# Who issues the loads of V's neighbouring rows in a block-sparse attention and FFN kernel: sync engine or GpSimd

## The chip, the cores and the metric

One core of one Trainium2 chip runs the whole program. The metric is device time in microseconds (us), the median of the runs. Engines are named as in the profile: PE (TensorE matmul), PEld (its weight loads), DVE (VectorE), ACT (ScalarE), POOL (GpSimd), SP (SyncE, which here only issues DMAs).

## What is computed

The reference is attention over blocks of 32 tokens followed by a two-matrix feed-forward net. It is cut here to its core:

```python
B, H, S, D = 4, 8, 768, 64          # 24 blocks of 32 tokens
scores = (q @ k.T) / sqrt(D)
mask = |blk_i - blk_j| <= 1  or  blk_i, blk_j in (first, last)  or  blk_j in sampled_blocks[blk_i]   # 3 per block
attn = softmax(where(mask, scores, -1e9))
x = (attn @ v).transpose(0, 2, 1, 3).reshape(B * S, H * D)      # 3072 x 512
out = leaky_relu(x @ w_in, 0.01) @ w_out                        # 512 -> 2048 -> 512
```

Inputs are f32, and the FFN weights come in a 64-bit type (the kernel reads them as pairs of 32-bit words and decodes them). Every f32 operand is split into a high and a low f16 part so that PE works in f16.

## The kernel before, in words

The program is one long list of instructions without loops at run time. The work is cut by batch b (4), by query tile T (12 of 64 queries each: tile 0 holds the first and the last block and sees all keys, tiles 1 to 11 hold two inner blocks) and by pair of heads hp (4). Four tiles make an item of 256 queries, and each item's attention output goes through the FFN later.

For an inner tile the keys and values are put together in 12 slots of 32 rows, 384 rows in all. Slots 0 to 3 are the four neighbouring blocks, contiguous in memory. Slots 4 to 9 are the sampled blocks, and slots 10 and 11 are the first and the last block. For K this is done in SBUF: DVE copies the neighbours (L631), POOL copies the six sampled blocks (`kg`, L640, each after a register load L639). For V it is done by DMA out of a scratch tensor `scr[b]` in DRAM, which holds V of that batch as f16 high and low parts, one row of 2048 bytes for each token (written by SP at L496 from `prep_v`).

`gather_v(b, T)` fills one of two buffers `vg` (128 partitions x 3 chunks x 2048 bytes), used in turn:

- L659: chunk 0, the 128 neighbouring rows, a plain DMA of 256 KB, for every inner tile (44 times);
- L663: the first and the last block into chunk 2, 32 rows each, only the first time that a buffer is used for a batch (16 times);
- L666: two indirect DMAs by GpSimd with the row numbers in `rows`, 128 rows into chunk 1 and 64 rows into chunk 2 (88 times).

A buffer can be refilled when the attention-times-V matmuls (`av`, L798) of the tile that used it are done; both the plain and the indirect loads wait for that.

What sets the order: the kernel writes its instructions down step by step with priorities, and the framework's scheduler then makes one fixed order for each engine out of dependencies, priorities and its own estimate of durations. Each engine works through its list strictly in order, so an instruction that waits holds up all that stands behind it on that engine. SP's list holds all plain loads and stores and all transposes by DMA: weights (L344), q and k (L516, L526), v (L465), the transposes of k (L558), of q (L583, followed by the two swapped copies `qxs`, L586 and L587) and of the probabilities (`pt`<-`pp`, L771). POOL's list holds the `kg` copies, the indirect loads, for item 0 the diagonal matrices `pp` (L738) with which PE transposes probabilities (`turn`, L756), and later the low half of the FFN's hidden values (`g`, L847).

Other lines that the prediction speaks of: the decoding of weights on ACT (L351) and DVE (L352, L353, L355), their split into halves on ACT (L414) and DVE (L419), the masked scores on DVE (`p`, `mx`, L706), the low half of q (`qa_q`, L580) and of the probabilities (`pt` at L760 for item 0, `pp` at L766 after it), the FFN matmuls on PE (`h` L833, `o` L860). The load of a piece of the weights is ordered behind the latest `pt` transpose on SP (L345).

Of the kernel before, what the change touches and what calls it, by code (L numbers as in the profile page):

```python
# [19 lines left out]
P = 128  # L20
# [48 lines left out]
def tile_block_sparse_attention_ffn(  # L69
# [19 lines left out]
    nc = tc.nc  # L89
# [369 lines left out]
    vscale, vraw, v16s, scr, vg = {}, {}, {}, {}, {}  # L459
# [194 lines left out]
    def gather_v(b, T):  # L654

        n = (b * (NT - 1) + T - 1) % 2
        vg = vgb[n]
        t0 = (T - 1) * Q2
        nc.sync.dma_start(out=vg[:, 0, :], in_=scr[b][t0:t0 + P, :])  # L659
        if vends.get(n) != b:  # L660
            vends[n] = b
            for i, at in enumerate((0, S - BLOCK)):
                nc.sync.dma_start(  # L663
                    out=vg[Q2 + i * BLOCK:Q2 + (i + 1) * BLOCK, 2, :], in_=scr[b][at:at + BLOCK, :])
        for c, n_ in ((1, P), (2, Q2)):
            nc.gpsimd.indirect_dma_start(  # L666
                out=vg[:n_, c, :], out_offset=None, in_=scr[b][:, :],
                in_offset=bass.IndirectOffsetOnAxis(ap=rows[:n_, c - 1, T - 1:T], axis=0))
        vgs[b, T] = vg.rearrange("p c (h x) -> p c h x", h=H)
# [364 lines left out]
    def start_gather_v():  # L1034
        b, T = vq.popleft()
        until(("v", b), lambda: (b, "ready") in scr)
        assert vfree[0] > 0
        if not b and T == 1:
            build_rows()
        vfree[0] -= 1  # L1040
        gather_v(b, T)
# [73 lines left out]
    for u in units:  # L1115
        it, ui = u.item, u.k * NP + u.hp
        b, nb = it.b, it.b + 1
# [172 lines left out]
```

## Time and profile before

| what | value |
| --- | --- |
| median of the runs | 863.69 us |
| the profiled execution, whole | 867.32 us |
| its span (first to last instruction) | 865.6 us |
| PE busy | 745.7 us (86%) |
| DVE busy | 601.8 us (70%) |
| ACT busy | 509.9 us (59%) |
| POOL busy | 356.3 us (41%), of it 94.2 in the 88 indirect loads |
| queue of SP (hardware_dynamic) | 116.74 MB, 64.9% of 16 DMA engines' span |
| queue of POOL (software_dynamic) | 17.31 MB, 8.2% |

How to read it: the profile gives for each engine its busy time and, in views by window, how that is spread over the span. The view of waits says for an idle stretch which instruction ended it ("engine line waited for: us in total, times, longest us"; SPq and POOLq are the issuing queues). The timeline lists instructions in order: start, length, engine, line, operation, with the idle time before it and what ended it in square brackets. A row of an issuing queue has the time that the issue took, not the transfer.

### The profile page before, as it was taken

The page shows a single profiled execution, that of the slowest core. Times are in us where ns is not written, and L with a number is a line of the kernel's source. Part 1 is how long each engine was busy: PE and PEld are TensorE (multiplying, and loading weights), DVE is VectorE, ACT ScalarE, POOL GpSimd, SP SyncE. Part 2 cuts the span into 40 slices and gives each one's busy share as a digit, 9 for nine tenths or more (in the row PEclk, how much of TensorE's full clock was granted, in tenths as well). Part 3 has the DMA queues.
Part 4 walks back from the last instruction along what each step waited for, and adds up shares of the span by engine and source line. Part 5 has one row for each costly group of instructions (what it writes and reads, how often), then busy time and mean ns, then how long its engine had stood idle before and what let it go on. Part 6 is the DMA issues. An engine that isn't in the chain of part 4 may idle for free.

```text
span 865.6 us, 20081 instructions
## 1 busy us (share of the span) xinstructions
PE 745.7 (86%) x7140; PEld 494.9 (57%) x7140; DVE 601.8 (70%) x1595; ACT 509.9 (59%) x1183; POOL 356.3 (41%) x473
## 2 busy tenths in 40 slices
PE   1456667766998899998999989999999999999997
PEld 1245545443756565665666566666666666666674
DVE  4668998988968678757966777778667676663221
ACT  4556676775634667666656757667467566553211
POOL 0416744642125346345543554453434554532121
PEclk9968979887999999999999999999999999999999
DMA  9877489998648879898759899967678576566000
GB/s 205 162 225 237 160 191 230 234 216 181 137 104 145 172 163 211 160 170 147 194 124 177 159 162 203 199 133 183 144 131 175 116 158 148 120 139 86 26 2 25
DMA packets 312771, 135.33 MB, mean 156 GB/s; under 512 B 279773, under 2 KB 292062, under 8 KB 312670
## 3 DMA queue, kind: packets, MB, share of 16 engines
q1 hardware_dynamic: 307038, 116.74, 64.9%
q0 software_dynamic: 5632, 17.31, 8.2%
q8 instruction: 56, 0.92, 0.5%
q14 instruction: 45, 0.37, 0.1%
HBM read 65.58 MB, written 12.58 MB: 90 GB/s over the span
## 4 chain that ended last, share of the span: by engine, by line
PE 43%; DVE 20%; DMA 18%; ACT 8%; issue 5%; SPq 3%; POOL 1%; POOLq 1%; ACTq 0%; DVEq 0%
PE o L860 17%; PE h L833 17%; PE av L798 4%; PE s L697 4%; DMA kt<-k_k 3%; DVE pp L766 3%; ACT p L718 3%; DVE p L706 3%; DMA rq<-in_q_dram 3%; DMA qs_q<-qa_q 3%; DMA qxs_q<-qs_q 2%; DMA pt<-pp 2%; DMA wbuf<-in_moe_w_out_dram 2%; DVE ht L842 1%; DMA rk<-in_k_dram 1%
## 5 line engine op out<-in xcount | busy, mean ns | idle before, releaser
L860 PE MATMUL o<-W,g 128*128 128x512 f16 x1152 | 273.8, 383 | 9.3 <-DVE g L846 6.7
L833 PE MATMUL h<-x,W 128*128 128x256 f16 x2304 | 276.0, 277 | 1.9 <-ACT ht L839 1.9
L833 PEld LDWEIGHTS <-W 128*128 128x128 f16 x2304 | 223.9, 100 | 49.0 <-issue 14.2
L847 POOL TENSOR_TENSOR g<-ht,g 128x512 f16<-128x512 f32 x96 | 116.4, 1213 | 312.7 <-DVE g L846 279.1
L860 PEld LDWEIGHTS <-g 128*128 128x128 f16 x1152 | 108.2, 98 | 132.4 <-issue 15.0
L718 ACT ACTIVATE p<-p,mx 128x384 f32<-128x384 f32 x208 | 126.1, 607 | 98.0 <-DVE mx L706 66.7
L640 POOL COPY kg<-kt 128x256 f16 x264 | 133.1, 531 | 76.6 <-PE s L697 42.6
L766 DVE SCALAR_TENSOR_TENSOR pp<-p,r,pp 128x384 f16<-128x384 f32 x188 | 125.3, 694 | 33.1 <-ACT pp L745 32.4
L666 POOL DMA_INDIRECT vg<-scr,rows x88 | 94.2, 1071 | 69.5 <-PE av L798 47.4
L842 DVE SCALAR_TENSOR_TENSOR ht<-ht 128x512 f32<-128x512 f32 x96 | 67.8, 706 | 75.2 <-ACT ht L839 75.0
L706 DVE CUSTOM_DVE_ANT_0 p<-s,em,nsc 128x384 f32<-128x384 f32 x176 | 102.9, 610 | 21.9 <-PE s L697 17.3
L745 ACT ACTIVATE pp<-p,r 128x384 f16<-128x384 f32 x188 | 104.1, 604 | 17.1 <-DVE r L730 15.6
L798 PE MATMUL av<-pt,vg 128*64 128x128 f16 x2112 | 80.8, 225 | 19.7 <-DMA pt<-pp 13.6
L798 PEld LDWEIGHTS <-vg 128*64 128x64 f16 x2112 | 68.3, 112 | 49.1 <-issue 43.9
L839 ACT ACTIVATE ht<-h,gd 128x512 f32<-128x512 f32 x80 | 54.1, 677 | 63.9 <-PE h L833 51.0
L697 PE MATMUL s<-kg,qs_q 128*64 128x384 f16 x352 | 60.7, 343 | 21.5 <-DVE mx L706 21.2
L697 PE MATMUL s<-kg,qxs_q 128*64 128x384 f16 x352 | 60.0, 336 | 6.1 <-DMA qxs_q<-qs_q 6.1
L697 PEld LDWEIGHTS <-qs_q 128*64 128x64 f16 x416 | 26.9, 110 | 55.5 <-issue 43.5
L846 DVE CAST g<-ht 128x512 f16<-128x512 f32 x96 | 42.3, 441 | 10.3 <-PE o L860 8.3
L730 DVE RECIPROCAL r<-sum 128x2 f32<-128x2 f32 x96 | 15.4, 160 | 36.3 <-ACT sum L729 35.6
L718 ACT ACTIVATION_READ_ACCUMULATOR p<-p,mx 128x1 f32 x208 | 39.1, 188 | 0.0
L571 ACT ACTIVATE qa_q<-rq 128x512 f16<-128x512 f32 x25 | 15.7, 628 | 38.8 <-DMA rq<-in_q_dram 38.8
(136 smaller groups left out, 762.1 us busy)
## 6 DMA issues: line engine op xcount, KB each, us to landing
vg<-scr SPq DMA_DIRECT2D x44, 256.0 KB, 3.8
qxs_q<-qs_q SPq DMA_DIRECT2D x48, 128.0 KB, 2.6
v<-in_v_dram SPq DMA_DIRECT2D x32, 192.0 KB, 4.8
scr<-v SPq DMA_DIRECT2D x16, 384.0 KB, 4.7
W<-in_moe_w_in_dram SPq DMA_DIRECT2D x5, 1024.0 KB, 9.4
rq<-in_q_dram SPq DMA_DIRECT2D x20, 256.0 KB, 6.1
out_dram<-ob SPq DMA_DIRECT2D x20, 256.0 KB, 3.1
rk<-in_k_dram SPq DMA_DIRECT2D x24, 192.0 KB, 4.7
```

The source lines that it names most:

```text
L640: nc.gpsimd.tensor_copy(out=kg[:, :, slot * BLOCK:(slot + 1) * BLOCK], in_=kt[:, :, bass.ds(off, BLOCK)])
L666: nc.gpsimd.indirect_dma_start(out=vg[:n_, c, :], out_offset=None, in_=scr[b][:, :], in_offset=bass.IndirectOffsetOnAxis(ap=rows[:n_, c - ...
L697: nc.tensor.matmul(o, a, k, start=(n == 0), stop=(n == 1)))
L706: nc.vector.tensor_tensor_reduce(out=u.p[i], in0=u.sp[i], in1=kgs[u.b, u.T][1] if u.T else zero.to_broadcast([P, KEYS]), scale=u.nsc, scal ...
L718: nc.scalar.activation(u.p[i], u.p[i], AF.Exp, scale=-1.0, bias=u.mx[:, :1], accum_out=u.pair.sum[:, u.pi, i:i + 1])
L745: nc.scalar.activation(pp[:, 0, :], p, AF.Copy, scale=u.r)
L766: nc.vector.scalar_tensor_tensor(out=pp[:, 1, :], in0=p, scalar=u.r, in1=pp[:, 0, :], op0=ALU.mult, op1=ALU.subtract)
L798: nc.tensor.matmul(o, a, m, start=(c == 0 and l == 0), stop=(c == n - 1 and l == 1)))
L833: nc.tensor.matmul(c.ph[:, i], w, x, start=(d == 0 and m == 0), stop=(d == NP - 1 and m == 2)))
L842: nc.vector.scalar_tensor_tensor(out=c.t, in0=c.t, scalar=0.01, in1=c.t, op0=ALU.mult, op1=ALU.max)
L847: nc.gpsimd.tensor_tensor(out=c.g[:, 1], in0=c.t, in1=c.g[:, 0], op=ALU.subtract)
L860: nc.tensor.matmul(o, a, w, start=(c.first and i == 0 and m == 0), stop=(c.last and i == 1 and m == 2)))
```

## The change

Three lines of `gather_v`: the neighbouring rows and the two end blocks are issued by GpSimd instead of the sync engine. Bytes, buffers, shapes and dependencies stay as they are.

```diff
         t0 = (T - 1) * Q2
-        nc.sync.dma_start(out=vg[:, 0, :], in_=scr[b][t0:t0 + P, :])
+        nc.gpsimd.dma_start(out=vg[:, 0, :], in_=scr[b][t0:t0 + P, :])
         if vends.get(n) != b:
             vends[n] = b
             for i, at in enumerate((0, S - BLOCK)):
-                nc.sync.dma_start(
+                nc.gpsimd.dma_start(
                     out=vg[Q2 + i * BLOCK:Q2 + (i + 1) * BLOCK, 2, :], in_=scr[b][at:at + BLOCK, :])
```

60 issues leave SP's list and join POOL's. Since the scheduler makes its order anew, other instructions change places as well; the order in which FFN matmuls stand between the attention tiles on PE is nearly the same.

First place: POOL at the first two gathers of batch 0 (T = 1 and 2). `vg_100` and `vg_101` are the two buffers, `scr_564` the scratch of batch 0, `pp_...<-eye` the diagonals for PE's transposes, and rows L639 (register loads) between the copies. Before:

```order
L738 TENSOR_SCALAR pp_0_0_3_511<-eye_88,r_0_0_2_490 128x128
L666 DMA vg_100<-scr_564,rows 128x1024
L666 DMA vg_100<-scr_564,rows 64x1024
L666 DMA vg_101<-scr_564,rows 128x1024
L666 DMA vg_101<-scr_564,rows 64x1024
L640 ISA
L640 COPY kg_98<-kt_136 128x8x32
```

and now:

```order
L738 TENSOR_SCALAR pp_0_0_3_511<-eye_88,r_0_0_2_490 128x128
L659 DMA vg_100<-scr_564 128x1024
L663 DMA vg_100<-scr_564 32x1024 x2
L666 DMA vg_100<-scr_564,rows 128x1024
L666 DMA vg_100<-scr_564,rows 64x1024
L659 DMA vg_101<-scr_564 128x1024
L663 DMA vg_101<-scr_564 32x1024 x2
L666 DMA vg_101<-scr_564,rows 128x1024
L666 DMA vg_101<-scr_564,rows 64x1024
L640 ISA
L640 COPY kg_98<-kt_136 128x8x32
```

Ten issues in a row instead of four stand ahead of the `kg` copies and, behind five of these, of the next diagonals.

Second place: DVE at the first scores of tile T = 2, which wait for PE's transposes and so for those diagonals (`W<-W,wi_s` is the split of a piece of the weights, `qa_q_1_0` the low half of q of item 1). Before:

```order
L154 RECIPROCAL wi_s<-wi_inv 128x1
L706 ISA p_0_2_0_0_765,mx_0_2_0_766<-s_0_2_0_0_719,em_2_715,nsc_0_1_0_717 128x384
L706 ISA mx_0_2_0_766 128x1
L154 RECIPROCAL q_1_0_s<-q_1_0_inv 128x1
L598 TENSOR_SCALAR nsc_1_0_0_1221<-kinv_132,q_1_0_inv 128x4
L816 TENSOR_TENSOR x_0_999<-xf_0_0_2_929,x_0_999 128x4x64
L706 ISA p_0_2_1_0_855,mx_0_2_1_856<-s_0_2_1_0_720,em_2_715,nsc_0_1_0_717 128x384
```

and now:

```order
L154 RECIPROCAL wi_s<-wi_inv 128x1
L154 RECIPROCAL q_1_0_s<-q_1_0_inv 128x1
L598 TENSOR_SCALAR nsc_1_0_0_1221<-kinv_132,q_1_0_inv 128x4
L816 TENSOR_TENSOR x_0_999<-xf_0_0_2_929,x_0_999 128x4x64
L419 SCALAR_TENSOR_TENSOR W<-W,wi_s 128x2x512
L580 SCALAR_TENSOR_TENSOR qa_q_1_0_830<-rq_1_0_668,q_1_0_s,qa_q_1_0_830 128x8x64
L706 ISA p_0_2_0_0_765,mx_0_2_0_766<-s_0_2_0_0_719,em_2_715,nsc_0_1_0_717 128x384
```

One split of weights and the low half of q now stand ahead of the scores, where they stood behind them.

Third place: SP from the weight loads behind the first gathers on. Before:

```order
L659 DMA vg_101<-scr_564 128x1024
L663 DMA vg_101<-scr_564 32x1024 x2
L344 DMA W<-in_moe_w_in_dram 128x2x1024
L344 DMA W<-in_moe_w_out_dram 128x2x1024
L344 DMA W<-in_moe_w_in_dram 128x2x1024
L583 DMA_TRANSPOSE qs_q_1_0_968<-qa_q_1_0_830 128x8x128
```

and now:

```order
L496 DMA scr_564<-v_0_3_729 128x6x256
L344 DMA W<-in_moe_w_in_dram 128x2x1024
L344 DMA W<-in_moe_w_out_dram 128x2x1024
L583 DMA_TRANSPOSE qs_q_1_0_968<-qa_q_1_0_830 128x8x128
L516 DMA rq_1_1_973<-in_q_dram 128x8x64
L586 DMA qxs_q_1_0_970<-qs_q_1_0_968 64x1024
L587 DMA qxs_q_1_0_970<-qs_q_1_0_968 64x1024
L344 DMA W<-in_moe_w_in_dram 128x2x1024 x2
```

The issues for `vg` are gone, and the third load of weights has moved behind the transpose and the copies of q.

## The prediction

> **What bounds the kernel now.** I read the page's busy tenths first, then windows cut where they change, then the waits of PE, and last the timeline where PE still waits. The tenths (40 slices of about 21.6 us):
>
> ```profile
> PE   1456667766998899998999989999999999999997
> DVE  4668998988968678757966777778667676663221
> ```
>
> PE is short of work for about ten slices and full from there on, while DVE is fullest in slices 4 to 9. The windows say the same in numbers:
>
> ```profile
> core 0: us, PE busy (x) PEld busy (x) DVE busy (x) ACT busy (x) POOL busy (x), PEclk, DMA share, GB/s
> ...
> 60.00:75.00 15.00, 12.72 (x123) 10.30 (x124) 10.92 (x36) 8.98 (x21) 9.48 (x14) 0.75 0.80 251
> 75.00:100.00 25.00, 14.75 (x163) 11.60 (x163) 24.66 (x45) 18.13 (x41) 16.20 (x20) 0.93 0.57 185
> 100.00:125.00 25.00, 15.44 (x191) 11.76 (x190) 25.00 (x72) 17.36 (x37) 15.77 (x18) 0.80 0.65 158
> 125.00:250.00 125.00, 97.29 (x894) 64.69 (x892) 108.09 (x274) 82.95 (x182) 43.29 (x48) 0.90 0.91 198
> 250.00:600.00 350.00, 326.58 (x3229) 212.74 (x3228) 255.14 (x679) 224.91 (x545) 160.76 (x224) 0.99 0.82 163
> 600.00:865.60 265.60, 258.90 (x2416) 169.18 (x2414) 144.88 (x366) 128.05 (x301) 98.81 (x125) 1.00 0.53 109
> ```
>
> From 75 to 125 us DVE works 49.66 of 50 us (it decodes weights and does the scores), from 125 to 250 still 108.09 of 125. After 250 us PE sets the pace: it idles 350 - 326.58 = 23.4 us and 265.6 - 258.9 = 6.7 us. PE's work is fixed and full at the end, so the end moves by as much as the start of that full stretch moves. What happens before 250 us counts; what happens after it counts only where PE itself waits. PE's waits, from 60 to 250 us and behind it:
>
> ```profile
> PE av L798 <- DMA pt<-pp: 13.6, 7, 4.7
> ...
> PE turn L756 <- POOL pp L738: 2.5, 3, 1.4
> ...
> PE turn L756 <- POOL kg L640: 1.8, 1, 1.8
> ...
> PE s L697 <- DMA qxs_q<-qs_q: 1.7, 2, 0.9
> ```
>
> ```profile
> PE s L697 <- DMA qxs_q<-qs_q: 4.4, 4, 1.9
> ...
> PE av L798 <- DMA pt<-pp: 3.1, 3, 1.8
> ...
> PE o L860 <- POOL g L847: 0.7, 1, 0.7
> ```
>
> No row has PE waiting for `vg`: the transfers that the change touches are early enough. What can move the time is their issuing, by freeing SP or by loading POOL.
>
> **What it takes off SP.** The issues themselves are short, and their cost to SP is the wait for `av` in front of them, since SP is in order. Over the span, and from 60 to 250 us:
>
> ```profile
> SPq L659 <- PE av L798: 89.7, 23, 14.5
> ```
>
> ```profile
> SPq L659 <- PE av L798: 28.6, 4, 14.5
> ```
>
> 61.1 of the 89.7 us lie outside the stretch from 60 to 250 us, where SP has to serve a PE that is nearly full anyway. Of the 28.6 us, the largest part is one place:
>
> ```profile
> 86.58 0.43 SPq L344 DMA_DIRECT2D wbuf<-in_moe_w_out_dram  x1
> 101.33 11.37 SPq L659 DMA_DIRECT2D vg<-scr  x2
> 113.13 1.96 SPq L771 DMA_TRANSPOSE pt<-pp  x1
> 115.14 1.00 SPq L344 DMA_DIRECT2D W<-in_moe_w_in_dram  x1
> ```
>
> ```profile
> 112.50 0.60 DVE L766 SCALAR_TENSOR_TENSOR pp<-p,r,pp 128x384 f16<-128x384 f32 x1
> ```
>
> SP stands from 87 to 112.7 us behind two loads for `vg`. Next in its list is the transpose of `pp`, and DVE finishes that `pp` only at 113.1; the weight load behind it is ordered behind that transpose by the code. So freeing SP here gains nothing: the wait for `av` becomes a wait for `pp` of the same end. Term: 0. Its bounds are 0 and the whole of what PE waits for `pt` and `qxs` behind 60 us, 13.6 + 1.7 + 4.4 + 3.1 = 22.8 us; I take the end that the one long wait shows, and keep the other for a rival.
>
> One load moves the wrong way. The third of these weight loads was issued at 68.62, and now stands behind the transpose of q:
>
> ```profile
> 68.62 0.47 SPq L344 DMA_DIRECT2D W<-in_moe_w_in_dram  x1
> 80.98 1.24 SPq L583 DMA_TRANSPOSE qs_q<-qa_q  x1
> ```
>
> ```profile
> 87.75 1.14 ACT L351 ACTIVATE W<-W 128x1024 f32<-128x1024 f32 x1 [1.02 <-DVE W L355]
> ```
>
> Its decoding starts on ACT no earlier than 87.75, and what that waits for is DVE, not the load. I put it at 0, since the decoding moves later by the term below; without that cover it would cost the few us by which the load then lands too late.
>
> **What it puts on POOL.** The trace before has no plain load issued by POOL. The nearest row is the indirect issue of the same engine into the same buffer; the issues by SP bound it from below:
>
> ```profile
> L666 POOL DMA_INDIRECT vg<-scr,rows x88: 899/1000/1943, 62.9 to 788.4; - x88
> L659 SPq DMA_DIRECT2D vg<-scr x44: 326/356/1367, 62.0 to 786.7; - x44
> L663 SPq DMA_DIRECT2D vg<-scr x16: 372/420/1542, 62.4 to 650.8; - x16
> ```
>
> Where it matters most is the first double gather, because work that others wait for is queued behind it:
>
> ```profile
> 62.90 1.33 POOL L666 DMA_INDIRECT vg<-scr,rows  x1 [3.39 <-issue]
> ...
> 67.23 1.64 POOL L666 DMA_INDIRECT vg<-scr,rows  x1 [0.31 <-issue]
> 68.88 1.76 POOL L640 COPY kg<-kt 128x256 f16 x5
> 70.63 1.18 POOL L738 TENSOR_SCALAR pp<-eye,r 128x128 f32<-128x128 f32 x2
> ```
>
> ```profile
> 71.28 2.93 PE L756 MATMUL turn<-pp,p 128*128 128x128 f32 x12 [0.93 <-POOL pp L738]
> ```
>
> ```profile
> 72.97 0.62 DVE L706 CUSTOM_DVE_ANT_0 p<-s,em,nsc 128x384 f32<-128x384 f32 x1 [1.71 <-PE turn L756]
> ...
> 75.26 1.28 DVE L419 SCALAR_TENSOR_TENSOR W<-W,wi_s 128x1024 f16<-128x1024 f32 x1
> ...
> 80.16 0.73 DVE L580 SCALAR_TENSOR_TENSOR qa_q<-rq,q_s,qa_q 128x512 f16<-128x512 f32 x1
> ```
>
> This reads as a chain: four issues, then the `kg` copies and the diagonals, for which PE waits 0.93 us, for which DVE waits 1.71 us. Four issues take 68.88 - 62.90 = 5.98 us, 1.5 us each with the gap between. Six more join them in front of the diagonals: two of 128 rows at 1.5 and four of 32 rows at the shortest indirect issue plus the gap, 0.90 + 0.31 = 1.2. Together 2 x 1.5 + 4 x 1.2 = 7.8 us. Bounds: 6 x 0.4 = 2.4 us, if POOL were as quick as SP, and 6 x (1.94 + 0.31) = 13.5 us, if each took as long as the longest indirect issue. I take 7.8, as the nearest row is one on the same engine.
>
> What covers it: the new order puts one split of weights (1.28) and the low half of q (0.73) in front of the scores on DVE, 2.0 us of useful work while it waits. Left: 5.8 us by which DVE enters its full stretch later, and DVE has no slack up to 125 us to make it good.
>
> After that, batch 0 has nine more gathers up to 208 us, each with one more issue:
>
> ```profile
> 206.94 0.97 POOL L666 DMA_INDIRECT vg<-scr,rows  x1 [8.62 <-PE av L798]
> ```
>
> At the mean of 1.07 us (94.2 us for 88) and 0.31 of gap this is 9 x 1.38 = 12.4 us of POOL. POOL already stands and waits for `av` there (8.62 us here), and that wait only moves from the first indirect issue to the plain one. Queued behind are `kg` copies, diagonals and, later, `g`. The rows of PE's waits give POOL 2.5 + 1.8 us in four places, of which one is the 0.93 above: three places could grow by 1.38 each. DVE is full then, so I charge 1.0 of the 4.1 us. Without DVE's backlog all 4.1 and in the worst case all 12.4 us would count. Given back: from 125 to 250 us DVE idles 125 - 108.09 = 16.9 us; some of these holes are waits for work that does not move, and I let them swallow 1.5 us. Behind 250 us, 33 gathers with 45 more issues fall on a POOL that is busy 160.76 of 350 us, and PE waits 0.7 us for it in all: 0. The bytes and the DMA engines stay the same: 0.
>
> **Sum:** 7.8 - 2.0 + 1.0 - 1.5 + 0 + 0 = +5.3 us. The profiled execution took 867.32 us and would take 872.6; it lies 3.6 us over the median, so against 863.69 the forecast is **869.0 us**, slower by 0.6%. A measurement of this kernel can tell about 2% (17.3 us) from no change, so this would count as no change.
>
> **The rivals.**
>
> *A, hidden:* DVE's 16.9 us of holes between 125 and 250 us swallow all of it, since the decoding chain there is partly paced by weight loads. For it: the holes are three times 5.3. Against: those loads are ordered behind `pt` transposes, which move with the rest. Time: 863.7.
>
> *B, SP freed (faster):* with 60 issues less on SP, `pt` and `qxs` arrive earlier, and half of PE's 22.8 us of waits for them go: -11.4, so 852.3. It decides from the point where a transpose is ready while SP still waits for `av`. For it: 89.7 us of SP's time stand in this wait. Against: the longest such wait ends together with the `pp` that the next transpose needs. To be 17.3 us faster it would need three quarters of the 22.8.
>
> *C, POOL becomes the bound in the weight stage (slower):* every one of the 15 added issues of batch 0 lands on the path, 7.8 + 12.4 = 20.2, so 883.9. It decides once a gather makes `kg` or the diagonals later than DVE has other work for, which is when DVE shows more than 1.4 us of idle time at each gather between 75 and 208 us. Against: DVE idles 0.34 us from 75 to 125.
>
> *D, starved issues:* DVE holds POOL's issues up. The longest indirect issue took 1.943 us against a shortest of 0.899, so some of them already wait for something. At that length the first double gather costs 13.5 instead of 7.8, and the sum becomes 13.5 - 2.0 + 1.0 - 1.5 = +11.0: 874.7. For it: DVE is fuller in this stage than elsewhere. Against: the median is 1.000, so most are not held up. [...]
>
> **How the numbers follow.** Chances: the forecast 0.45, A 0.20, B 0.14, D 0.12, C 0.09. The range reaches from B's 852 to just below C's end, **852 to 883**; the parts of B beyond half of the waits and of C at its full price are left out. Faster by over 2% (below 846.4) needs three quarters of B's waits or a lucky new order: 0.06. Slower by over 2% (above 881.0) is most of C and the tail of D: 0.10. Within 2%: 0.84.
>
> **What would show it.** Right: plain issues on POOL of 1.0 to 1.6 us, ten issues in a row from about 63 us to about 77, the diagonals and PE's `turn` behind them some 8 us later than 71.28, DVE idle 5 to 8 us there, and the full stretch of PE some 5 us later; SP's waits for `av` at L659 gone and most of them turned into waits for `pp` or `av` at L771. Wrong: PE's wait for `pt` falling well below 16.7 us (B), DVE idle beside each gather (C), plain issues near 2 us (D), or issues near 0.4 us, which would leave the first gather almost unchanged (2.4 - 2.0 = +0.4) and the time at A's.

## The result and the profile after

The changed kernel takes **898.64 us** (median of 4 runs, 896.15 to 900.38), beside 862.94 us of the kernel before on the same chip: ratio 1.0392, 95% interval [1.0332, 1.0452]. The ratio is taken over the fast runs of both kernels alone (one run of before took 2543.98 us) and is not the quotient of the two medians. The changed kernel is slower by 3.9%, outside the range of the prediction. The profiled execution took 896.15 us with a span of 894.3; the one of before 867.32 with 865.6. So 28.7 us of span are to be found.

First the page after: busy time of the engines, then the clock that TensorE was granted, in 40 slices.

```profile
PE 761.5 (85%) x7140; PEld 502.7 (56%) x7140; DVE 609.2 (68%) x1595; ACT 510.5 (57%) x1183; POOL 389.2 (44%) x533
...
PEclk9966968896999898989999999999999999989999
```

PE did the same 7140 matmuls and needed 761.5 us for them; the busy time of before was 745.7. So 15.8 of the 28.7 us are PE's own work at a lower clock (granted 0.941 in the mean of the span, 0.963 before), and only 12.9 are idle time. Next the windows, with the cuts of the prediction:

```profile
60.00:75.00 15.00, 10.28 (x112) 8.10 (x110) 11.10 (x32) 8.86 (x21) 11.72 (x19) 0.84 0.73 243
75.00:100.00 25.00, 17.63 (x162) 13.28 (x162) 21.47 (x44) 14.63 (x33) 16.33 (x23) 0.71 0.60 185
100.00:125.00 25.00, 12.74 (x160) 9.01 (x160) 25.00 (x63) 19.25 (x42) 12.50 (x18) 0.84 0.41 86
125.00:250.00 125.00, 97.88 (x891) 64.20 (x892) 111.67 (x279) 79.91 (x175) 46.46 (x56) 0.87 0.93 199
250.00:600.00 350.00, 320.58 (x3083) 209.16 (x3082) 235.68 (x640) 212.75 (x515) 168.43 (x236) 0.96 0.82 156
600.00:894.30 294.30, 281.85 (x2602) 183.69 (x2601) 171.13 (x416) 145.56 (x342) 122.00 (x160) 0.99 0.54 112
```

How far is the kernel behind at 250 us? FFN matmuls are PE's filler, so their count tells. The groups of PE from 0 to 250 us, before and after:

```profile
L833 PE MATMUL h<-x,W 128*128 128x256 f16 x312 | 39.5, 289 | 0.0
L860 PE MATMUL o<-W,g 128*128 128x512 f16 x126 | 34.0, 411 | 8.5 <-DVE g L846 6.7 <-ACT ob L878 1.8
```

```profile
L833 PE MATMUL h<-x,W 128*128 128x256 f16 x277 | 35.5, 290 | 0.7 <-DVE x L816 0.6
L860 PE MATMUL o<-W,g 128*128 128x512 f16 x120 | 32.3, 417 | 1.6 <-DVE g L846 1.4 <-POOL g L847 0.2
```

35 matmuls of 39.5/312 and 6 of 34.0/126 us are missing: 6.0 us. The number is near what the prediction had expected of this stretch (5.3); the experiments show that this is no confirmation of its terms. Behind 250 us it had expected nothing, and there stands the rest. PE's idle time was 23.4 + 6.7 = 30.1 us and is 29.4 + 12.45 = 41.9: 11.8 more. Its busy time there grew from 585.5 to 602.4, by 17.0: 6.0 of it is the work left over, the other 11 go with the clock, 0.96 instead of 0.99 over 350 us and 0.99 instead of 1.00 over the rest. Idle time and busy time together give the 28.7 us.

What PE waits for between 250 and 470 us, before and after (total us, times, longest):

```profile
PE s L697 <- DVE mx L706: 6.4, 5, 2.5
PE h L833 <- ACT ht L839: 1.9, 2, 1.2
PE av L798 <- DMA pt<-pp: 1.8, 1, 1.8
```

```profile
PE av L798 <- DMA pt<-pp: 13.7, 8, 3.8
PE s L697 <- DVE mx L706: 3.3, 5, 1.4
PE k_sum L131 <- ACT k_k L540: 2.2, 1, 2.2
```

PE now comes to `av` eight times before the transposed probabilities are there, where it came once. One of the two longest of these waits in the timeline (the other, 3.80 us, ends at 295.36), and the clock in windows of 3.4 us around it:

```profile
368.29 0.33 PE L697 MATMUL s<-kg,qxs_q 128*64 128x384 f16 x2
...
376.63 1.90 PE L860 MATMUL o<-W,g 128*128 128x512 f16 x8
...
379.52 1.47 SPq L771 DMA_TRANSPOSE pt<-pp  x1
...
383.12 0.33 PE L697 MATMUL s<-kg,qxs_q 128*64 128x384 f16 x2
...
387.23 0.71 PE L798 MATMUL av<-pt,vg 128*64 128x128 f16 x9 [3.77 <-DMA pt<-pp]
387.87 3.59 PE L860 MATMUL o<-W,g 128*128 128x512 f16 x8
```

```profile
379.60:383.00 3.40, 3.40 (x31) 2.42 (x30) 1.58 (x4) 2.55 (x7) 2.66 (x4) 1.00 1.24 182
383.00:386.40 3.40, 0.45 (x6) 0.08 (x2) 2.52 (x7) 3.40 (x9) 0.45 (x1) 1.00 1.03 114
386.40:389.80 3.40, 2.57 (x14) 1.23 (x15) 0.00 (x0) 0.72 (x5) 0.70 (x1) 0.51 1.14 224
389.80:393.20 3.40, 3.40 (x23) 1.71 (x22) 0.00 (x0) 1.37 (x2) 0.00 (x0) 0.50 1.48 148
```

The `av` at 387.23 needs the probabilities of the scores that end at 368.62; SP issued their transpose at 379.52. Between these scores and this `av` PE's list holds 64 FFN matmuls, where the kernel before holds 180 for the same tile (356 to 391.5 us). PE is through with them and with the scores of a later tile (383.12) before the transpose has landed. It stands 3.77 us, with 0.45 us of work in the window from 383.00, and in the two windows behind it the granted clock is 0.51 and 0.50: eight matmuls of `o` take 3.59 us instead of 1.90. This stall is paid twice, as idle time and as slow work behind it. Cut into slices of 2 us, the stretch from 250 us on has six places where the granted clock falls to between 0.50 and 0.57, each right behind a wait of PE of 2.1 to 3.8 us; before had three, at 0.50 to 0.55 behind waits of 1.9 to 2.5 us. Summed over all the slices, 1 minus the granted clock, times the length, comes to 17.1 us, and to 5.1 before.

The engine that took over the loads, by lines and op (duration min/median/max in ns), and the first double gather:

```profile
L659 POOL DMA_DIRECT2D vg<-scr x44: 572/604/792, 62.0 to 816.4; - x44
...
L663 POOL DMA_DIRECT2D vg<-scr x16: 511/558/587, 62.8 to 664.7; - x16
...
L666 POOL DMA_INDIRECT vg<-scr,rows x88: 903/993/1951, 64.2 to 818.9; - x88
```

```profile
62.05 0.79 POOL L659 DMA_DIRECT2D vg<-scr  x1 [3.17 <-DMA scr<-v]
62.84 1.09 POOL L663 DMA_DIRECT2D vg<-scr  x2
64.23 1.05 POOL L666 DMA_INDIRECT vg<-scr,rows  x1 [0.30 <-issue]
...
70.71 1.77 POOL L640 COPY kg<-kt 128x256 f16 x5
72.47 1.19 POOL L738 TENSOR_SCALAR pp<-eye,r 128x128 f32<-128x128 f32 x2
```

```profile
73.13 2.93 PE L756 MATMUL turn<-pp,p 128*128 128x128 f32 x12 [3.56 <-POOL pp L738]
```

A plain issue took GpSimd 0.6 us, not 1.2 to 1.5. Ten issues take 70.71 - 62.05 = 8.66 us, 2.7 more than the four of before; PE's `turn` starts at 73.13 instead of 71.28, and its wait for the diagonals has grown from 0.93 to 3.56 us. And SP's waits, before and after:

```profile
SPq L771 <- PE av L798: 72.7, 21, 7.7
SPq L771 <- DVE pp L766: 66.8, 36, 4.3
```

```profile
SPq L771 <- DVE pp L766: 140.1, 45, 28.3
SPq L771 <- PE av L798: 99.4, 31, 7.7
```

The waits at L659 are gone, and SP waits at its transposes instead, 100.0 us more in these two rows. SP is freed of them; what that is worth is tested below.

### The profile page after: what moved, and what is told of

The parts are those of the page before. It is cut to its first block, busy times and chain, and to the rows that moved or that the text cites. A ratio compares the mean times of both kernels' runs of the same rounds, so it can differ in the third digit from the quotient of the medians.

```text
span 894.3 us, 20082 instructions
## 1 busy us (share of the span) xinstructions
PE 761.5 (85%) x7140; PEld 502.7 (56%) x7140; DVE 609.2 (68%) x1595; ACT 510.5 (57%) x1183; POOL 389.2 (44%) x533
## 3 DMA queue, kind: packets, MB, share of 16 engines
q0 software_dynamic: 9664, 29.89, 13.0%
## 4 chain that ended last, share of the span: by engine, by line
PE 46%; DVE 20%; DMA 16%; ACT 8%; issue 5%; SPq 3%; POOL 2%; POOLq 1%; ACTq 0%; DVEq 0%
PE h L833 19%; PE o L860 18%; PE av L798 4%; PE s L697 4%; DMA pt<-pp 3%; DVE pp L766 3%; DVE p L706 3%; DMA kt<-k_k 3%; ACT p L718 3%; DMA qs_q<-qa_q 3%; DMA qxs_q<-qs_q 2%; DMA rq<-in_q_dram 2%; DVE ht L842 2%; DVE W L419 1%; DVE W L353 1%
## 5 line engine op out<-in xcount | busy, mean ns | idle before, releaser
L833 PE MATMUL h<-x,W 128*128 128x256 f16 x2304 | 282.5, 280 | 1.0 <-DVE x L816 0.6
L860 PE MATMUL o<-W,g 128*128 128x512 f16 x1152 | 278.2, 387 | 3.6 <-DVE g L846 1.6
L833 PEld LDWEIGHTS <-W 128*128 128x128 f16 x2304 | 226.8, 101 | 54.0 <-issue 14.5
L860 PEld LDWEIGHTS <-g 128*128 128x128 f16 x1152 | 109.3, 99 | 128.2 <-issue 16.9
L640 POOL COPY kg<-kt 128x256 f16 x264 | 131.3, 524 | 91.8 <-PE s L697 56.2
L766 DVE SCALAR_TENSOR_TENSOR pp<-p,r,pp 128x384 f16<-128x384 f32 x188 | 128.0, 712 | 29.7 <-ACT pp L745 25.9
L842 DVE SCALAR_TENSOR_TENSOR ht<-ht 128x512 f32<-128x512 f32 x96 | 69.7, 726 | 66.4 <-ACT ht L839 66.0
L666 POOL DMA_INDIRECT vg<-scr,rows x88 | 92.0, 1045 | 28.8 <-issue 25.0
L697 PE MATMUL s<-kg,qs_q 128*64 128x384 f16 x352 | 61.6, 349 | 23.4 <-DVE mx L706 22.8
L659 POOL DMA_DIRECT2D vg<-scr x44 | 26.7, 606 | 60.7 <-PE av L798 57.3
L697 PEld LDWEIGHTS <-qxs_q 128*64 128x64 f16 x416 | 25.4, 114 | 28.9 <-DMA qxs_q<-qs_q 23.9
```

The source lines that it names most:

```text
L640: nc.gpsimd.tensor_copy(out=kg[:, :, slot * BLOCK:(slot + 1) * BLOCK], in_=kt[:, :, bass.ds(off, BLOCK)])
L666: nc.gpsimd.indirect_dma_start(out=vg[:n_, c, :], out_offset=None, in_=scr[b][:, :], in_offset=bass.IndirectOffsetOnAxis(ap=rows[:n_, c - ...
L697: nc.tensor.matmul(o, a, k, start=(n == 0), stop=(n == 1)))
L766: nc.vector.scalar_tensor_tensor(out=pp[:, 1, :], in0=p, scalar=u.r, in1=pp[:, 0, :], op0=ALU.mult, op1=ALU.subtract)
L833: nc.tensor.matmul(c.ph[:, i], w, x, start=(d == 0 and m == 0), stop=(d == NP - 1 and m == 2)))
L842: nc.vector.scalar_tensor_tensor(out=c.t, in0=c.t, scalar=0.01, in1=c.t, op0=ALU.mult, op1=ALU.max)
```

## The experiments

A change of this kind does two things at once: another engine issues, and the scheduler makes all orders anew. **Theories** at the start: O, the new order costs; I, the issuing itself costs; M, half of each. For the issuing there were later three ways (S, GpSimd's time in front of other work; H, SP is no longer held back and issues other things at other moments; R, the loads travel beside the transposes, on GpSimd's queue, which moved 29.89 MB in the changed kernel and 17.31 before). To hold an order, each kernel called "held" below chains the instructions of every engine, as one of the kernels had them, by dependencies without a semaphore:

```diff
+    traced = list(nc.cur_bb.bb.instructions)
+    for packed in ORDER.values():
+        row = np.frombuffer(zlib.decompress(base64.b85decode(packed)), '<u2').tolist()
+        for a, b_ in zip(row, row[1:]):
+            tc.add_manual_dep(traced[b_], traced[a].name, mybir.DependencyInfo(
+                mybir.DependencyClass.NoSync, mybir.DependencyReason.DATA), reason="pinned")
```

Ratios are to the kernel before on the same chip (its median lay between 862.9 and 867.9 us), with 95% intervals. Of the runs below only `pool_busy` lies beyond 2% with its whole interval; the effects of about 1% are read as effects where the interval leaves out 1.

**Order and issuer apart.** `before_pinned`: before, held in its own order.

> The kernel before with its own order pinned: nothing but the pinning. All theories: within 0.5% of before, 859 to 867 us; another time would mean that pinning itself has a price, and the two other runs would be read against it.

Measured: 869.36 us, 1.0011 [0.9964, 1.0058]. Holding an order costs nothing that shows.

`sp_new_order`: before's code, held in the changed kernel's order; the loads stay on SP behind their old neighbours.

> The sync engine issues the 60 loads as before, but every engine's list is pinned to the order of the changed kernel (the loads stand in SP's list behind the same instruction as before). Theory O: 888 to 905 us, like the changed kernel. Theory I: 860 to 870. Theory M: about 880.

Measured: 891.85 us, 1.0266 [1.0187, 1.0345].

`pool_old_order`: the changed code, held in before's order, each moved load directly ahead of the first indirect issue of its gather.

> GpSimd issues the 60 loads as in the change, but every engine's list is pinned to the order of the kernel before (the moved loads stand directly ahead of the first indirect load of their gather). Theory O (the scheduler's new order is what costs): 860 to 870 us, within 1% of before. Theory I (issuing by GpSimd costs: its queue, its descriptors, its traffic beside the transposes): 885 to 900 us. Theory M (half each): about 880.

Measured: 888.06 us, 1.0238 [1.0156, 1.0320]. Both cost, the first as theory O and the second as theory I had said, and they do not add up: 2.7 and 2.4 against 3.9 together.

`only_neighbours`: only the 44 loads of neighbouring rows move, the scheduler orders.

```diff
-                nc.gpsimd.dma_start(
+                nc.sync.dma_start(
                     out=vg[Q2 + i * BLOCK:Q2 + (i + 1) * BLOCK, 2, :], in_=scr[b][at:at + BLOCK, :])
```

> One part of the change alone, ordered by the scheduler: the 44 loads of neighbouring rows by GpSimd, the 16 small loads of the end blocks by the sync engine. Theory I: 44 of 60 issues, so about 26 of the 36 us: 885 to 893. Theory O: a third order, its time anywhere between 855 and 905 and not in proportion to the number of issues.

Measured: 877.21 us, 1.0083 [1.0034, 1.0131]. Three quarters of the loads, and a fifth of the loss; theory I had said 885 to 893.

**Where in time the order costs.** `new_order_early` and `new_order_late`: SP issues, one order up to the instruction that PE of before reached at 250 us, the other behind it.

> SP issues all loads. Every engine's instructions up to the one that TensorE of before reached at 250 us stand in the changed kernel's order, all later ones in the order of before. The new order cost some 24 us with SP issuing (891.9 against 868). If that arises in the later attention tiles (L): 868 to 876, since only some 5 us of lag stand at 250 us in the changed kernel. If the early part sets it (E): about 888.

> The other half: the order of before up to that instruction, the changed kernel's order behind it, SP issuing all loads. L: 882 to 890, with TensorE idle and at half clock more behind 250 us. E: 868 to 873.

Measured: early 872.40 us, 1.0066 [1.0027, 1.0104]; late 885.98 us, 1.0232 [1.0155, 1.0309]. L holds: most of the order's cost arises where the prediction had put 0. The early part alone costs some 5.7 us with SP issuing, about as much as the 6.0 us by which the changed kernel lags at 250 us.

**Is any new order dear?** `sp_nb_order`: SP issues, held in the order of `only_neighbours`. `only_end_blocks`: only the 16 loads of L663 go to GpSimd, the scheduler orders. `order_nudge`: SP issues, and in batch 1 one line stands ahead of the load:

```diff
+        if b == 1:
+            nc.gpsimd.memset(vg[:, 0, :1], 0.0)
         nc.sync.dma_start(out=vg[:, 0, :], in_=scr[b][t0:t0 + P, :])
```

> Every engine in the order that the scheduler made for the kernel with only the 44 loads of neighbouring rows on GpSimd (877.2), but SP issues all 60 loads. If this order is as dear as that of the full change (some 24 us): 885 or more. If orders differ by chance and this one costs nothing, its kernel's 9 us came from the issuing alone: 862 to 870. In between, 872 to 878, the order carries them.

> Only the 16 loads of the end blocks go to GpSimd, in the order that the scheduler makes of it (2207 of 13899 rows on TensorE stand elsewhere than before, against 4930 in the full change and 3368 with the 44 others). The issuing is a quarter of the full change's, so at most 5 us. If a new order costs by itself, whatever brought it: 874 to 890. If only the full change's order is dear: 866 to 873.

> SP issues all loads. In batch 1 alone GpSimd writes one column of zeros into the buffer ahead of each load of neighbouring rows (11 writes of some 0.1 us, overwritten by the load), and the scheduler orders anew: 370 of 13899 rows on TensorE and 736 of 1567 on VectorE stand elsewhere. If any new order costs: 872 to 880. If small moves are harmless: 866 to 870.

Measured: 875.27 us, 1.0105 [1.0039, 1.0170]; 866.27 us, 0.9963 [0.9935, 0.9992]; 870.38 us, 1.0003 [0.9969, 1.0037]. So the theory that any new order costs has fallen: two are as good as the old one, one of them better by 0.4%, which is the fastest version of this study and by less than the 2% that one would call a gain. In the order of `only_neighbours` no difference shows between the issuers (1.0105 with SP, 1.0083 with GpSimd).

**What the dear order does.** I counted in the programs: for each tile `pt`, the FFN matmuls (L833, L860) in PE's list between the last scores that it comes from and the first `av` that reads it. They are the work that covers exponentials, split and transpose. Mean of 26 tiles of each batch:

```
order of            batch 1  batch 2  batch 3   ratio with SP issuing
before               131.3    141.5    145.2    1.0011
order_nudge          131.0    141.5    145.2    1.0003
only_end_blocks      128.2    141.5    145.2    0.9963 (16 loads on GpSimd)
only_neighbours      127.2    142.1    146.8    1.0105
the changed kernel    85.1    142.9    146.8    1.0266
```

Batch 1's attention (from its first scores to its last `av` 252 to 457 us before, 258 to 475 us now) lost a third of its cover, batches 2 and 3 none. This is where the eight waits for `pt` stand. Three kernels test it: `order_batch1` and `order_batch23` put only that stretch, or only what is behind it, into the changed kernel's order, SP issuing; `after_batch1_old` is the full change with before's order in that stretch alone.

> SP issues all loads; the order of before up to 250 us and from some 466 us on, the changed kernel's order only for the instructions that before ran in between, which are batch 1's attention. Theory C, cover: in the changed kernel TensorE has 85.1 matmuls of the FFN between the scores of two units of batch 1 and their av, against 131.3 before, and nearly the same number in batches 2 and 3; so av waits for pt. Then this kernel (85.1) keeps the whole late cost: 882 to 888. If the cost is spread over all late tiles (D): 872 to 878.

> SP issues all loads; the order of before up to some 466 us, the changed kernel's order behind it (batches 2 and 3). C: cover is 131.3, 141.8 and 146.8 as before, so 866 to 871. D: 876 to 884.

> The full change, GpSimd issuing all 60 loads, in its own order except between 250 and some 466 us, where every engine has the order of before (cover 131.3 instead of 85.1). C: the order's cost goes and the issuing's stays: 876 to 886, against 898.6 of the full change. D: 888 to 894.

Measured: 882.13 us, 1.0195 [1.0136, 1.0253]; 874.24 us, 1.0107 [1.0049, 1.0165]; 874.22 us, 1.0078 [1.0036, 1.0119]. PE's waits from 250 to 470 us in the first and in the last:

```profile
PE av L798 <- DMA pt<-pp: 13.5, 9, 5.6
PE av L798 <- DMA vg<-scr: 6.2, 1, 6.2
```

```profile
PE s L697 <- DVE mx L706: 5.9, 6, 1.9
PE s L697 <- DMA qxs_q<-qs_q: 3.5, 2, 1.8
PE av L798 <- DVE xf L808: 1.9, 2, 1.1
PE av L798 <- DMA pt<-pp: 1.7, 1, 1.7
```

and the windows of the last:

```profile
250.00:600.00 350.00, 325.44 (x3228) 212.57 (x3227) 255.02 (x680) 223.88 (x544) 178.70 (x254) 1.00 0.83 167
600.00:869.40 269.40, 258.30 (x2419) 169.20 (x2417) 149.26 (x367) 128.57 (x302) 108.43 (x141) 1.00 0.49 105
```

With batch 1's cover given back, the wait for `pt` falls from 13.7 to 1.7 us, the clock returns to 1.00, and the full change costs 0.8% instead of 3.9%. That is most of the result in one stretch of one order. Three limits to this. What was exchanged is the order of every engine in that stretch; that the cover is what counts in it is read off the waits and the table, since no kernel moves FFN matmuls alone. In `order_batch1` 6.2 us are a wait for `vg`, which the changed kernel does not have, so its 2.0% is not the price of the cover alone. And C expected `order_batch23` to be free, and it is not (1.1%); what costs there is not the cover, and stays open. C also expected the whole price of the issuing to stay in `after_batch1_old` (876 to 886); 874.22 lies just below.

**How the issuing costs.** With before's order held: `pool_sp_held` splits the load, so that SP waits at its old places,

```diff
-        nc.gpsimd.dma_start(out=vg[:, 0, :], in_=scr[b][t0:t0 + P, :])
+        nc.sync.dma_start(out=vg[:16, 0, :], in_=scr[b][t0:t0 + 16, :])
+        nc.gpsimd.dma_start(out=vg[16:, 0, :], in_=scr[b][t0 + 16:t0 + P, :])
```

and `pool_busy` leaves all loads on SP and gives GpSimd small work at each of their places; `pool_busy_light` does it once instead of three times:

```diff
+        moved = 1 if vends.get(n) == b else 3
...
+        for i in range(3 * moved):
+            nc.gpsimd.tensor_scalar(out=spare, in0=eye32[:, :32], scalar1=eye32[:, :1], scalar2=None, op0=ALU.mult)
```

> The order of before is held, GpSimd issues the two end blocks and rows 16 to 127 of the neighbouring rows, and SP issues rows 0 to 15 at its old places, so that SP waits there for av as it did before. Three theories of the 19 us that GpSimd's issuing cost with the order held (888.1 against 869.4): H, SP is no longer held back, and what it issues next reaches the DMA engines at other moments: then about 870 here. S, GpSimd loses 0.6 us to each issue: about 888. R, the loads travel on GpSimd's own queue, beside the transposes instead of in line with them: about 886.

> Before in its own order with SP issuing all loads; GpSimd does in addition, at each place where the change puts a load, three small multiplications of 128x32 into a spare tile, some 0.6 us together. S (GpSimd's time): about 888. H and R (what travels, and when): 867 to 872, as before.

> As pool_busy, with one small multiplication of some 0.5 us at each place of a moved load instead of three, so that GpSimd's added time is about that of the real issues (30 us in all), while all loads stay on SP. S, GpSimd's time carries the direct cost: 880 to 888. If only part of it: 872 to 880. R, the queue that the loads travel on carries it: 867 to 872.

Measured: 884.74 us, 1.0188 [1.0111, 1.0265]; 896.64 us, 1.0351 [1.0254, 1.0448]; 880.48 us, 1.0132 [1.0055, 1.0208]. H, which had said about 870, falls as the whole cause; the interval leaves room for a part of it. GpSimd's time alone does cost; in `pool_busy` it was more than meant, three multiplications of 0.505 us at a place where 0.6 together were expected:

```profile
L668 POOL TENSOR_SCALAR spare<-eye 128x32 f32<-128x32 f32 x180 | 90.8, 505 | 13.9 <-POOL kg L640 0.9 <-issue 0.3
```

90.8 us, where the 60 issues of the changed kernel take 44 x 0.606 and 16 x 0.550, or 35.5; so only the light one, with 32.6 us in 60 multiplications, is to be set beside them: 1.3% against 2.4%.

`pool_first` and `pool_rest`: GpSimd issues only batch 0's 15 loads, or only the other 45 (`load = nc.gpsimd if b == 0 else nc.sync`, and with `b > 0`).

> The order of before is held. GpSimd issues only the 15 moved loads of batch 0 (11 gathers, up to some 210 us), SP the other 45. GpSimd issuing all 60 in this order cost 19 us. The prediction's place for the cost is here: its terms give 7.8 - 2.0 + 1.0 - 1.5 = 5.3 us, about 875. If an issue is 0.6 us and the losses lie in the full stretch behind 250 us (L): 868 to 872.

> The complement: SP issues the 15 loads of batch 0, GpSimd the 45 of batches 1 to 3, in the order of before. The prediction puts this part at 0: 867 to 871. L, TensorE's stalls behind 250 us and the half-clock windows beside them: 878 to 888.

Measured: 874.73 us, 1.0107 [1.0070, 1.0143]; 875.08 us, 1.0074 [1.0032, 1.0117]. About 9 and 6 us, with intervals of 6.0 to 12.4 and 2.8 to 10.1: both parts cost, and which costs more can't be told. The second lies between what the prediction (867 to 871) and L (878 to 888) had said, so neither was met.

`pool_behind`: as `pool_old_order`, but each load stands behind the copies of `kg` and the diagonals that follow its gather.

> The order of before is held and GpSimd issues all 60 loads, but each stands as far back on GpSimd as the copies of kg and the diagonals behind its gather reach, in front of the next subtraction for g or the next gather. The same loads travel on the same queue; only what waits behind them on GpSimd is other. If the 0.6 us in front of the diagonals and the kg copies carry the cost (S): 866 to 874, and the first scores' turn starts as early as before. If the queue carries it (R), or what lies behind the loads does not matter: 880 to 889. A wait of av for vg would show the loads as too late.

Measured: 878.83 us, 1.0120 [1.0084, 1.0157]. The same loads on the same queue cost half as much when less work stands behind them on GpSimd; the time lies between what S and R had said. PE does not wait for `vg` here, so the loads are not too late. The other sign of S, a `turn` as early as before, came only in part: PE's wait there for GpSimd's diagonals is 0.94 us in `before_pinned`, 3.16 in `pool_old_order` and 2.31 here. Taken together, about half of the issuer's cost is S, by the means of two kernels that agree (1.3% from the time alone, 1.2% taken away by the place); the intervals allow from a quarter to most of it. For the rest R or a part of H is left of my three, and no run shows either by itself. All this holds for the order of before: in the changed kernel's order GpSimd's issuing adds some 1.3 points (3.9 against 2.7).

## Why the prediction was wrong, point by point

- **The bound (PE from 250 us on, DVE up to 125)** was right, and DVE's stretch from 100 to 125 us is full as before (25.00 of 25 us). What did not follow is that behind 250 us only those waits of PE would count that the trace before shows: PE was full there because of the order, which was about to change.
- **"SP freed: 0"** was right. SP waits at L771 instead. With the order held, PE's wait for `pt` from 60 to 250 us is the same with either issuer (14.0 us in `before_pinned`, 13.6 in `pool_old_order`). In the changed kernel it does fall there, to 3.6 us, but the new order does that with SP issuing too (6.4 in `sp_new_order`), and the waits for `qxs` and `mx` take the time back: 1.7 and 11.4 us before, 7.5 and 15.7 now. Rival B (852.3) was out, and A (863.7) with it.
- **First double gather, 7.8 us.** The mechanism was right, and the size was not: a plain issue is 0.6 us on GpSimd, between the two bounds of 0.4 and 2.25 and near the lower one; ten issues took 2.7 us more than four. The nearest row, the indirect issue of the same engine, was the wrong neighbour; SP's plain issue of 0.36 us was nearer. `turn` came 1.85 us later, not 8.
- **Cover of 2.0 us on DVE** stood as the order had it, the split and q's low half ahead of the scores; these start at 75.79 instead of 72.97 us:

```profile
73.61 1.48 DVE L419 SCALAR_TENSOR_TENSOR W<-W,wi_s 128x1024 f16<-128x1024 f32 x1 [0.44 <-ACT W L414]
75.01 0.85 DVE L580 SCALAR_TENSOR_TENSOR qa_q<-rq,q_s,qa_q 128x512 f16<-128x512 f32 x1
75.79 0.60 DVE L706 CUSTOM_DVE_ANT_0 p<-s,em,nsc 128x384 f32<-128x384 f32 x1
```

- **The nine later gathers of batch 0, 1.0, and 1.5 given back.** All of batch 0 cost 9 us in the held order ([6.0, 12.4] from the interval). The cover of 2.0 comes with the new order, so 7.8 + 1.0 - 1.5 = 7.3 is what the terms give here, within the interval. The sum came near by luck: its largest term was three times too big, and how issues of 0.6 us become 9 us there isn't resolved step by step. The 6.0 us of lag at 250 us do not bear the 5.3 out either, since the early part of the new order brings about as much with SP issuing (`new_order_early`).
- **"Behind 250 us ... 0" is the step that failed.** First in the issuing: "33 gathers with 45 more issues" cost 6 us in the held order. PE's wait for GpSimd of 0.7 us was read as the price; by which other waits the 6 us reach PE was not followed in a trace. Second and larger, in the order: the statement ahead of the prediction that the order of the FFN matmuls between the attention tiles is nearly the same was false for batch 1, where 131 became 85. The places shown there are those of the moved loads, in batch 0; nothing was said of the cover of the later batches. The order of batch 1's stretch costs 2.0% with SP issuing, and giving it back takes 3.1 of the 3.9 points off the full change.
- **No term for the clock.** The prediction took PE's work as fixed. In the changed kernel stalls of the full stretch are paid again in slow work behind them, at a granted clock down to 0.50 in six places: 11.8 us of added idle time came with about 11 us of slower work. Not every stall is: `after_batch1_old` idles 35.7 us behind 250 us, 5.6 more than before, with the clock at 1.00.
- **Rival D (starved issues):** not seen. The 60 plain issues took 0.511 to 0.792 us, none near 2, and the longest indirect one 1.951 as against 1.943. That VectorE holds issues of GpSimd up was a conjecture, and no row of the two traces shows it. **Rival C** named the right engine, but DVE idles only 3.5 us from 75 to 100 and none from 100 to 125, and the lag behind the weight stage was 6.0 us, not 20.2. A new order stood in the prediction only on the faster side ("a lucky new order"), not as a danger.

## What to carry to other kernels

When a scheduler orders the program, an edit is two edits: compare the new order where the bound lies, not where the edit lies, and count the filler matmuls between each producer of a long chain and its consumer on the engine that is full. Here 11.8 us more of idle time on a TensorE that is otherwise full came with about 11 us of slower work, at a granted clock down to 0.50 behind the waits, so waits behind the last bottleneck were not small change. Before an edit is blamed, hold the old order with the edit and the new order without it: here most of the loss went when the order of one stretch was given back.

## What the runs showed of the hardware

- In the changed kernel a plain DMA issue from GpSimd took 0.604 us for 128 rows and 0.558 for 32, by the medians above, against 0.993 for an indirect one. Four times the rows took 0.046 us more, and the longest of the 60 was 0.792, with VectorE busy for 68% of the span.
- One profiled execution does not carry 1%: `pool_first` took from 869.19 to 880.10 us in 11 runs with a median of 874.73, and its profiled one 879.41. So differences of some us between two profiles show where time goes, and only the ratios show how much.
